# Cosformer attention and a multiplicative feed-forward layer on one core: the output products of tiles 2 to 8 by seven block products in place of eight

## The chip, the cores and the metric

The kernel runs on one core of one Trainium2 chip, as one launch. The metric is the device time of that core in microseconds (us). The kernel before takes 253.65 us (median of 3 runs, 253.58 to 253.87). The span of a profile is a little shorter than the time, as it runs from the first to the last instruction.

## The reference

The first part is linear attention with cosine weights, of 8 batches, 8 heads, 576 positions and 64 features a head. The second is a feed-forward layer on the 4608 rows that result, with 512 columns in and out and 1024 inside.

```python
# attention, for each batch and head; c, s = cos, sin of pi/2 * position / 576
phi = lambda x: concatenate([relu(x) * c, relu(x) * s], axis=-1)
kv  = einsum('bhsf,bhsd->bhfd', phi(k), v)
num = einsum('bhsf,bhfd->bhsd', phi(q), kv)
den = einsum('bhsf,bhf->bhs', phi(q), phi(k).sum(axis=2)) + 1e-6
x   = (num / den)  # as 4608 rows of 512
# feed-forward
out = (((x @ w1) * (x @ w2)) @ w3) @ w_out
```

Inputs and output are float32; the kernel multiplies in bfloat16 and accumulates in float32.

## The kernel before

The kernel forms w34 = w3 @ w_out once on the chip, so the layer is out = ((x @ w1) * (x @ w2)) @ w34. The rows are worked off in nine tiles t = 0 to 8 of 512 rows. A tile first has eight pairs of products (index jc, 128 of the 1024 inner columns each): ScalarE copies the first of a pair from PSUM, VectorE multiplies it with the second into abT. Then comes the output stage of four row blocks `ms` of 128 rows. Tiles 0 and 1 have a variant of the first stage that is cut here.

```python
def ffn_tile():                                  # four PSUM banks, taken in turn
    pool = ps_ffn[ffn_tiles[0] // 2 % 2]         # two pools, bufs=2 each
    ffn_tiles[0] += 1
    return pool.tile([P, 512], FP32, name="ffnps")

def ffn_groups(t):
    abT = fsb.tile([P, 8, 512], BF16, name="abT", bufs=2)
    ...
    for jc in range(4 if t < 2 else 0, 8):
        aT = ffn_tile()
        products(aT[:, :], w1b, jc, slice(0, 512))       # 4 matmuls of 512 columns, L432
        asb = fsb.tile([P, 512], BF16, name="asb")
        nc.scalar.copy(out=asb[:], in_=aT[:, :])         # L469
        yield
        bT = ffn_tile()
        products(bT[:, :], w2b, jc, slice(0, 512))
        nc.vector.tensor_mul(out=abT[:, jc, :], in0=asb[:], in1=bT[:, :])   # L473
        yield
    ...
    for ms in range(3 if t == NT - 1 else 4):            # the output stage
        ops = ffn_tile()
        for jc in range(8):
            nc.tensor.matmul(ops[:, :], lhsT=abT[:, jc, ts(ms, 128)], rhs=w34b[:, jc, :],
                             start=(jc == 0), stop=(jc == 7))               # L486
            if jc == 3:
                yield
        if ms % 2 == 0:
            osb = holds[0].tile([P, 2, 512], FP32, name="osb")
            kept.append(osb)
        nc.scalar.copy(out=osb[:, ms % 2, :], in_=ops[:, :])                # L493
        if t == NT - 1:
            store(nc.sync, osb[:, ms % 2:ms % 2 + 1, :], 4 * t + ms, 1)
        yield
    # the last block of the last tile: two halves of 256 columns (L502), each stored at once
```

At each `yield` the program puts the attention work of later rows that the plan has for this slot: features of q and k (L259 on VectorE, L263 on ScalarE), the copy of v (L283, GpSimd), kv (L291), the numerators (L349) and their normalization on VectorE. A tile from t = 1 on has 24 slots: two for each jc and eight in the output stage. Every engine works its instructions off in the order in which the program gives them. The accumulators `pnum` of kv and of the numerators have one buffer of two banks. Attention ends with tile 6.

```python
def num(b, c, chain=True):
    ...
    nt = ps_att.tile([P, 2, 512], FP32, name="pnum")     # ps_att: bufs=1
    for h in range(H):
        nc.tensor.matmul(nt[:, h // 4, ds((h % 4) * 65, 65)], lhsT=qpT[:, h, ds(at, 128)],
                         rhs=kvs[:, h, :], start=True, stop=True)           # L349
    ...
    def normalize():
        nc.vector.tensor_scalar_add(out=den[rows], in0=n4[:, :, :, 64], scalar1=1e-6)   # L359
        nc.vector.reciprocal(out=den[rows], in_=den[rows])                              # L360
        nc.vector.tensor_tensor(out=xblk[rows], in0=n4[:, :, :, 0:D], in1=..., op=ALU.mult)  # L361

bases = [74, 99, 123, 148, 173]                          # slots of batches 4 to 7
for b, last, base in zip(range(4, B), bases, bases[1:]):
    plan_loads(b, [last + s for s in (-8, -5, 1, 4, 7, 10)])
    plan(b, kf=[last + s for s in (4, 7, 10, 13, 15)],   # features of k
         vc=[base + s for s in (-9, -8, -7, -6, -5)],    # copies of v
         kv=[base + s for s in (-4, -3, -3, -2, -2)],
         qf=[base + s for s in (-12, -9, -6, -3, 0)],    # features of q
         nu=[base + s for s in (0, 2, 5, 8, 11)])        # numerators
```

The outputs stay in the ten buffers `osb` (HELD) until their store is issued by GpSimd, at planned slots. Loads and stores on GpSimd come behind a small copy (`seen`, L521) that waits for a mark of ScalarE (L519), which keeps them from starting early.

Of the kernel before, what the change touches and what calls it, by code (L numbers as in the profile page):

```python
# [68 lines left out]
def kernel(  # L69
# [11 lines left out]
    nc = tc.nc  # L81
# [4 lines left out]
    NT = T // 512  # L86

    const = ctx.enter_context(tc.tile_pool(name="const", bufs=1))
# [46 lines left out]
    w34b = const.tile([P, 8, DM], BF16, name="w34b")  # L135
# [255 lines left out]
    def rows_of(b, c, n):  # L391

        if b == 0:
            if c == 4:
                return [out[512:S, :].rearrange("(p j) m -> p j m", j=1)]
            return [out[0:512, :].rearrange("(p j) m -> p j m", j=4)[:, c:c + n, :]]
        lower = out[ds(b * S, 320), :].rearrange("(p j) m -> p j m", j=5)
        upper = out[ds(b * S + 320, 256), :].rearrange("(p j) m -> p j m", j=4)
        return [h[:, c:c + n, :] for h in ((lower,) if c == 4 else (lower, upper))]

    def store(eng, osb, g, n, cols=slice(0, DM)):

        pair, r = divmod(g, 9)
        b, c = (2 * pair, r) if r < 4 else (2 * pair + 1, r - 5)
        if r == 4:
            parts = rows_of(2 * pair, 4, 1) + rows_of(2 * pair + 1, 4, 1)
        elif n == 1 or c + n <= 4:
            parts = rows_of(b, c, n)
        else:
            parts = None  # L410
        if parts is None or (r == 4 and n > 1):
            for i in range(n):
                store(eng, osb[:, i:i + 1, :], g + i, 1, cols)
            return
        for i, rows in enumerate(parts):
            on = eng[i % 2] if isinstance(eng, tuple) else eng
            on.dma_start(out=rows[:, :, cols], in_=osb[64 * i:64 * i + rows.shape[0], :, cols])  # L417

    ffn_tiles = [0]

    def ffn_tile():
        pool = ps_ffn[ffn_tiles[0] // 2 % 2]
# [4 lines that stand above are left out]
        x = xT[t]  # L427
        abT = fsb.tile([P, 8, 512], BF16, name="abT", bufs=2)

        def products(out, w, jc, tok):  # L430
            for kc in range(4):
                nc.tensor.matmul(out, lhsT=w[:, kc, ts(jc, 128)], rhs=x[:, kc, tok],  # L432
                                 start=(kc == 0), stop=(kc == 3))

        def on_half(half):

            for pair in range(2):
                a, b = ffn_tile(), ffn_tile()
                if pair == 0 and t == 0:
                    for quarter in range(2):  # L440
                        for i in range(2):
                            for ps, w in ((a, w1b), (b, w2b)):
                                products(ps[:, ds(256 * i + 128 * quarter, 128)], w, i,
                                         ds(256 * half + 128 * quarter, 128))
                            if half == 0 and quarter == 0 and i == 0:
                                yield
                        if quarter == 0:
                            yield
                else:
                    for ps, w in ((a, w1b), (b, w2b)):  # L450
                        for i in range(2):
                            products(ps[:, ts(i, 256)], w, 2 * pair + i, ts(half, 256))
                        if w is w1b and (t == 1 or half == 0):
                            yield
                asb = fsb.tile([P, 512], BF16, name="asb")
                nc.scalar.copy(out=asb[:], in_=a[:, :])
                nc.vector.tensor_mul(out=abT[:, ts(pair, 2), ts(half, 256)],
                                     in0=asb[:].rearrange("p (i n) -> p i n", i=2),
                                     in1=b[:, :].rearrange("p (i n) -> p i n", i=2))
                yield  # L460

        if t < 2:
            yield from on_half(0)
            yield from on_half(1)
        for jc in range(4 if t < 2 else 0, 8):
            aT = ffn_tile()
            products(aT[:, :], w1b, jc, slice(0, 512))
# [3 lines that stand above are left out]
            bT = ffn_tile()  # L471
            products(bT[:, :], w2b, jc, slice(0, 512))
            nc.vector.tensor_mul(out=abT[:, jc, :], in0=asb[:], in1=bT[:, :])  # L473
            yield
        if t == 0:
            for jp in range(8):
                for part in range(2):
                    w34_mm(jp, part)
                    yield
            early.close()  # L480
            holds.append(ctx.enter_context(tc.tile_pool(name="hold", bufs=HELD,
                                                        reuse_waits="tile")))
        for ms in range(3 if t == NT - 1 else 4):
            ops = ffn_tile()
            for jc in range(8):
# [12 lines that stand above are left out]
            for half in range(2):  # L498
                cols = ts(half, 256)
                ops = ffn_tile()  # L500
                for jc in range(8):
                    nc.tensor.matmul(ops[:, 0:256], lhsT=abT[:, jc, ts(3, 128)],  # L502
                                     rhs=w34b[:, jc, cols], start=(jc == 0), stop=(jc == 7))
                nc.scalar.copy(out=osb[:, 1, cols], in_=ops[:, 0:256])
                store((nc.sync, nc.scalar), osb[:, 1:2, :], 4 * t + 3, 1, cols)
                yield


    HELD = 10
    holds, kept = [], []  # L510
    slots = [[] for _ in range(40 + 24 * (NT - 1))]

    def at(s, *calls):
        slots[s] += calls

    def hold_back():

        mark = sm.tile([P, 1], BF16, name="mark", bufs=8)
        nc.scalar.copy(out=mark[0:1, :], in_=zeros[0:1, 0:1])  # L519
        seen = sm.tile([P, 1], BF16, name="seen", bufs=1)  # L520
        nc.gpsimd.tensor_copy(out=seen[0:1, :], in_=mark[0:1, :])  # L521
# [13 lines left out]
    def plan_loads(b, when):  # L535

        for piece, s in zip([(n, half) for n in "kqv" for half in range(2)], when):
            def issue(piece=piece):
                hold_back()
                load(b, *piece)  # L540
            at(s, issue)
# [57 lines left out]
    for b, last, base in zip(range(4, B), bases, bases[1:]):  # L599
        plan_loads(b, [last + s for s in (-8, -5, 1, 4, 7, 10)])  # L600
        plan(b, kf=[last + s for s in (4, 7, 10, 13, 15)],
             vc=[base + s for s in (-9, -8, -7, -6, -5)],
             kv=[base + s for s in (-4, -3, -3, -2, -2)],
             qf=[base + s for s in (-12, -9, -6, -3, 0)],
             nu=[base + s for s in (0, 2, 5, 8, 11)])

    for i in range(2 * (NT - 1)):
        def put(i=i):
            hold_back()
            store(nc.gpsimd, kept[i][:, :, :], 2 * i, 2)  # L610
# [3 lines left out]
    for t in range(NT):  # L614
        for _ in ffn_groups(t):
            for u in slots[g]:
                u()
            g += 1
# [31 lines left out]
```

## Time and profile before

| | before |
|---|---|
| time | 253.65 us (253.58 to 253.87) |
| span of the profile | 251.3 us, granted TensorE clock 1.00 |
| TensorE, VectorE, ScalarE, GpSimd busy | 240.8, 139.0, 130.5, 94.3 us |
| output products L486, L502 | 271 recorded of 280, and 16 |
| output stages of tiles 2 to 8 begin at | 103.6, 127.1, 150.8, 174.2, 197.9, 219.4, 239.9 us |
| spans of tiles 2 to 8 | 23.4, 24.0, 23.7, 23.3, 23.3, 20.9, 25.1 us |

The spans are cut where the first products of each tile begin, at 87.6, 111.0, 135.0, 158.7, 182.0, 205.3 and 226.2 us; that of tile 8 has the end of the program in it. In the profile PE is TensorE, PEld its weight loads, DVE VectorE, ACT ScalarE, POOL GpSimd; L486 is line 486 of the kernel. A group's row has the number of instructions, their busy time, the mean duration of one in ns, and the idle time of the engine just before them with what ended it. Durations of matmuls overlap, so the pace of matmuls is taken from the distance of their starts. The slices divide the span into forty parts, each digit the busy share in tenths.

### The profile page before, as it was taken

The numbers are of one execution on the slowest core, as the hardware profiler recorded it, in microseconds if no ns is written. First come the engines' busy times: TensorE is split into PE (matmuls) and PEld (weight loads), VectorE is DVE, ScalarE is ACT, GpSimd is POOL, SyncE is SP. The second block draws the span as 40 slices with busy tenths as digits, with TensorE's granted clock in tenths as the row PEclk, the third lists the DMA queues.
The fourth block names the chain that finished last, engine by engine and source line by source line (L and its number), as shares of the span: only waits on it lengthen the run. The fifth ranks groups of instructions, "written<-read, shape, count | busy, mean of one in ns | idle before, by whom it ended". The sixth has DMA issues, their size and how long they took to land.

```text
span 251.3 us, 5013 instructions
## 1 busy us (share of the span) xinstructions
PE 240.8 (96%) x1838; PEld 130.7 (52%) x1867; DVE 139.0 (55%) x331; ACT 130.5 (52%) x269; POOL 94.3 (38%) x197
## 2 busy tenths in 40 slices
PE   8889999999999999999999999999999999999993
PEld 2578555565874445454544545454545444444442
DVE  7775663637878445649565475567475644303310
ACT  2676324686843783466556644854575333334322
POOL 7764240232242344128032712382233009785000
PEclk9999999999999999999999999999999999999999
DMA  6999999899999999999999999999998447997015
GB/s 194 185 194 200 210 204 204 112 121 148 140 146 183 176 148 138 145 149 166 154 179 181 187 136 174 189 168 143 187 172 162 95 45 194 273 314 246 0 42 125
DMA packets 83895, 41.02 MB, mean 163 GB/s; under 512 B 51488, under 2 KB 80416, under 8 KB 83872
## 3 DMA queue, kind: packets, MB, share of 16 engines
q0 software_dynamic: 35456, 27.20, 70.4%
q1 hardware_dynamic: 48256, 13.38, 37.6%
q8 instruction: 14, 0.23, 0.4%
q10 hardware_dynamic: 160, 0.13, 0.2%
q14 instruction: 9, 0.07, 0.1%
HBM read 38.80 MB, written 9.44 MB: 192 GB/s over the span
## 4 chain that ended last, share of the span: by engine, by line
PE 77%; DMA 13%; DVE 4%; issue 2%; POOL 1%; ACT 1%; ACTq 0%; POOLq 0%; DVEq 0%
PE ffnps L432 41%; PE ffnps L486 24%; DMA w3b<-in_moe_w_dram 6%; PE pnum L349 4%; PE pnum L291 4%; PE ffnps L226 3%; DMA w2b<-in_moe_w_dram 3%; DMA qs<-in_q_dram 3%; DVE xblk L361 2%; DVE abT L473 1%; PE pst L214 1%; PE pst L322 1%; DVE den L360 1%; PE pst L387 0%; DVE qp L259 0%
## 5 line engine op out<-in xcount | busy, mean ns | idle before, releaser
L432 PE MATMUL ffnps<-xT,w2b 128*128 128x512 bf16 (+2 forms) x332 | 74.6, 348 | 0.3
L432 PE MATMUL ffnps<-xT,w1b 128*128 128x512 bf16 (+2 forms) x323 | 73.6, 347 | 0.8 <-DVE xT L389 0.3
L473 DVE TENSOR_TENSOR abT<-asb,ffnps 128x512 bf16<-128x512 bf16 x64 | 43.9, 686 | 48.4 <-PE ffnps L432 46.1
L469 ACT CAST asb<-ffnps 128x512 bf16<-128x512 f32 x64 | 37.3, 583 | 52.5 <-PE ffnps L432 48.7
L486 PE MATMUL ffnps<-w34b,abT 128*128 128x512 bf16 x271 | 63.7, 379 | 0.5
L521 POOL COPY seen<-mark 1x1 bf16<-1x1 bf16 x52 | 10.3, 197 | 96.8 <-ACT mark L519 96.8
L432 PEld LDWEIGHTS <-w1b 128*128 128x128 bf16 x336 | 30.4, 98 | 26.8 <-issue 0.8
L432 PEld LDWEIGHTS <-w2b 128*128 128x128 bf16 x336 | 30.5, 98 | 26.6
L486 PEld LDWEIGHTS <-abT 128*128 128x128 bf16 x280 | 26.1, 98 | 28.2 <-DVE abT L473 0.2
L493 ACT COPY osb<-ffnps 128x512 f32<-128x512 f32 x35 | 20.5, 585 | 35.4 <-PE ffnps L486 35.3
L263 ACT ACTIVATE qp<-qs,sinv 128x512 bf16<-128x512 bf16 (+2 forms) x40 | 28.0, 715 | 1.6 <-DMA qs<-in_q_dram 1.6
L361 DVE TENSOR_TENSOR xblk<-pnum,den 128x512 bf16<-128x512 f32 (+1 forms) x39 | 26.9, 691 | 1.4
L263 ACT ACTIVATE kp<-ks,sinv 128x512 bf16<-128x512 bf16 (+1 forms) x35 | 24.8, 717 | 2.6 <-DMA ks<-in_k_dram 2.6
L417 POOL DMA_DIRECT2D out_dram<-osb x42 | 22.3, 536 | 3.4 <-issue 3.0
L283 POOL COPY va<-vs 128x512 bf16<-128x512 bf16 (+1 forms) x30 | 17.8, 629 | 11.9 <-DMA vs<-in_v_dram 11.9
L259 DVE TENSOR_SCALAR qp<-qs,cosv 128x512 bf16<-128x512 bf16 (+1 forms) x40 | 19.4, 493 | 2.8 <-DMA qs<-in_q_dram 2.8
L349 PEld LDWEIGHTS <-qpT 128*128 128x128 bf16 x320 | 14.9, 98 | 10.1 <-issue 1.9
L359 DVE TENSOR_SCALAR den<-pnum 128x8 f32<-128x8 f32 (+1 forms) x39 | 6.4, 164 | 24.3 <-PE pnum L349 24.2
L349 PE MATMUL pnum<-kvs,qpT 128*128 128x65 bf16 x312 | 16.4, 194 | 0.7 <-DVE xblk L361 0.3
L226 PE MATMUL ffnps<-woutb,w3T 128*128 128x512 bf16 x62 | 14.8, 379 | 0.1
L291 PEld LDWEIGHTS <-kp 128*128 128x128 bf16 x280 | 11.4, 98 | 4.1
L259 DVE TENSOR_SCALAR kp<-ks,cosv 128x512 bf16<-128x512 bf16 (+1 forms) x35 | 12.0, 353 | 2.5 <-DMA ks<-in_k_dram 2.5
(83 smaller groups left out, 180.0 us busy)
## 6 DMA issues: line engine op xcount, KB each, us to landing
out_dram<-osb POOLq DMA_DIRECT2D x16, 256.0 KB, 4.4
out_dram<-osb POOLq DMA_DIRECT2D x24, 128.0 KB, 3.7
qs<-in_q_dram POOLq DMA_DIRECT2D x9, 256.0 KB, 7.9
ks<-in_k_dram POOLq DMA_DIRECT2D x7, 320.0 KB, 6.9
qs<-in_q_dram POOLq DMA_DIRECT2D x7, 320.0 KB, 6.9
vs<-in_v_dram POOLq DMA_DIRECT2D x7, 320.0 KB, 6.5
ks<-in_k_dram POOLq DMA_DIRECT2D x7, 256.0 KB, 7.8
vs<-in_v_dram POOLq DMA_DIRECT2D x7, 256.0 KB, 5.5
```

The costliest lines, as they stand in the source:

```text
L226: nc.tensor.matmul(acc[:, :], lhsT=w3T[:, lc, :], rhs=woutb[:, lc, :], start=(lc == 0), stop=(lc == 7))
L259: nc.vector.tensor_scalar(out=dst[:R, c, :, 0:D], in0=src[:R, :, c, :], scalar1=0.0, scalar2=cosv[:R, at:at + 1], op0=ALU.max, op1=ALU.mult)
L263: nc.scalar.activation(out=dst[:R, c, 0:n, D:F], in_=src[:R, 0:n, c, :], func=ACTF.Relu, scale=sinv[:R, at:at + 1], bias=0.0)
L291: nc.tensor.matmul(kvt[:, h // 4, ds((h % 4) * 65, 65)], lhsT=kp[:, c, h, :], rhs=va[:, c, h, 0:D + 1], start=(i == 0 and h % 4 == 0), sto ...
L349: nc.tensor.matmul(nt[:, h // 4, ds((h % 4) * 65, 65)], lhsT=qpT[:, h, ds(at, 128)], rhs=kvs[:, h, :], start=True, stop=True)
L361: nc.vector.tensor_tensor(out=xblk[rows], in0=n4[:, :, :, 0:D], in1=den[rows].unsqueeze(3).to_broadcast([R, 2, 4, D]), op=ALU.mult)
L417: on.dma_start(out=rows[:, :, cols], in_=osb[64 * i:64 * i + rows.shape[0], :, cols])
L432: nc.tensor.matmul(out, lhsT=w[:, kc, ts(jc, 128)], rhs=x[:, kc, tok], start=(kc == 0), stop=(kc == 3))
L469: nc.scalar.copy(out=asb[:], in_=aT[:, :])
L473: nc.vector.tensor_mul(out=abT[:, jc, :], in0=asb[:], in1=bT[:, :])
L486: nc.tensor.matmul(ops[:, :], lhsT=abT[:, jc, ts(ms, 128)], rhs=w34b[:, jc, :], start=(jc == 0), stop=(jc == 7))
L493: nc.scalar.copy(out=osb[:, ms % 2, :], in_=ops[:, :])
```

## The change

One level of Strassen's scheme is put on the output product of tiles 2 to 8. The four row blocks of a tile are taken as two pairs (a = 0, 1). For each pair abT is a matrix of two by two blocks (rows 0 and 1 of the pair; inner columns 0 to 511 and 512 to 1023), and w34 is one of two by two blocks (inner rows; output columns 0 to 255 and 256 to 511). Eight block products of 4 matmuls of 256 columns each would be what the kernel before computes; the scheme needs seven, of sums of blocks, and adds the results up. It is for less work on TensorE; sums take its place on the other engines:

- five sums of blocks of w34 (`wsum`), once, by VectorE, in tile 2;
- sums of blocks of abT in each tile, behind jc = 1, 3 (GpSimd, from tile 7 on VectorE) and behind jc = 5, 6, 7 (VectorE), two of them in place;
- sums of the products for each pair, on VectorE out of PSUM, and for tiles before 7 two subtractions on GpSimd. Three of the seven products are accumulated in the PSUM bank of an earlier one after that has been read.

The number of slots of a tile stays. The diff, with blank lines and the passage that gives each product its operands cut:

```diff
+    wsum = {i: const.tile([P, 4, 256], BF16, name=f"wsum{i}") for i in (1, 3, 4, 6, 7)}
+    asum = {i: const.tile([P, 4, 2, P], BF16, name=f"asum{i}") for i in (1, 5, 6)}
...
+    def product_sums(t, abT, lo, hi):
+        v = abT[:].rearrange("p j (a h n) -> p j a h n", a=2, h=2)
+        a11, a21 = (v[:, lo % 4:(hi - 1) % 4 + 1, :, h, :] for h in range(2))
+        a12, a22 = (v[:, 4 + lo % 4:4 + (hi - 1) % 4 + 1, :, h, :] for h in range(2))
+        n = slice(lo % 4, (hi - 1) % 4 + 1)
+        if lo < 4:
+            eng = nc.gpsimd if t < BUSY else nc.vector
+            eng.tensor_tensor(out=asum[6][:, n], in0=a21, in1=a11, op=ALU.subtract)
+            return
+        for out, in0, in1, op in ((asum[1][:, n], a11, a22, ALU.add),
+                                  (asum[5][:, n], a11, a12, ALU.add),
+                                  (a21, a21, a22, ALU.add), (a12, a12, a22, ALU.subtract)):
+            nc.vector.tensor_tensor(out=out, in0=in0, in1=in1, op=op)
...
+            b3, b6 = ffn_tile(), ffn_tile()
+            product(b3, 3, True)
+            nc.scalar.copy(out=c12, in_=b3[:, 0:256])
+            product(b6, 6, True)
+            yield
+            b4, b1 = ffn_tile(), ffn_tile()
+            product(b4, 4, True)
+            add(c11, c12, b4[:, 0:256])
+            product(b1, 1, True)
+            add(c22, c11, b1[:, 0:256])
+            yield
+            product(b3, 5, False)
+            nc.scalar.copy(out=c12, in_=b3[:, 0:256])
+            put(0, ts(1, 256))
+            product(b4, 2, False)
+            nc.scalar.copy(out=c21, in_=b4[:, 0:256])
+            put(1, ts(0, 256))
+            if t < BUSY:
+                add(c11, c11, c12, ALU.subtract, nc.gpsimd)
+                add(c22, c22, c21, ALU.subtract, nc.gpsimd)
+            else:
+                add(c11, c11, b3[:, 0:256], ALU.subtract)
+                add(c22, c22, b4[:, 0:256], ALU.subtract)
+                add(c22, c22, b6[:, 0:256])
+                put(1, ts(1, 256))
+            yield
+            product(b1, 7, False)
+            add(c11, c11, b1[:, 0:256])
+            put(0, ts(0, 256))
+            if t < BUSY:
+                add(c22, c22, b6[:, 0:256])
+            yield
...
+            if by_seven(t) and jc in (1, 3, 5, 6, 7):
+                product_sums(t, abT, jc - (jc < 6), jc + 1)
...
+        if by_seven(t):
+            yield from out_by_seven(t, abT)
+            return
...
+    SEVEN, BUSY = 2, 7
...
+    for i, s in zip((3, 6, 4, 1, 7), (66, 68, 70, 73, 76)):
+        at(s, lambda i=i: weight_sum(i))
```

`product` is four matmuls of 256 columns, `add` one sum of 128 x 256 float32 on VectorE unless an engine is named, `put` stores a piece in the last tile and does nothing before it, and `by_seven(t)` is true from tile 2 on. `weight_sum` is one VectorE instruction on two blocks of w34 of 128 x 1024.

More of the change, by code (lines that the diff above doesn't have):

```diff
@@ L417, in store, with w34_block, weight_sum @@
             on.dma_start(out=rows[:, :, cols], in_=osb[64 * i:64 * i + rows.shape[0], :, cols])
+    wsum = {i: const.tile([P, 4, 256], BF16, name=f"wsum{i}") for i in (1, 3, 4, 6, 7)}
+    asum = {i: const.tile([P, 4, 2, P], BF16, name=f"asum{i}") for i in (1, 5, 6)}
+    def w34_block(row, col):
+        return w34b[:, ts(row, 4), ts(col, 256)]
+    def weight_sum(i):
+        (r0, c0), (r1, c1), op = {1: ((0, 0), (1, 1), ALU.add), 3: ((0, 1), (1, 1), ALU.subtract),
+                                  4: ((1, 0), (0, 0), ALU.subtract), 6: ((0, 0), (0, 1), ALU.add),
+                                  7: ((1, 0), (1, 1), ALU.add)}[i]
+        nc.vector.tensor_tensor(out=wsum[i][:], in0=w34_block(r0, c0), in1=w34_block(r1, c1), op=op)
@@ new lines, in by_seven @@
+    def by_seven(t):
+        return t >= SEVEN
+    def product_sums(t, abT, lo, hi):
[11 more added lines that the diff above has]
+            nc.vector.tensor_tensor(out=out, in0=in0, in1=in1, op=op)
@@ new lines, in out_by_seven, with lhs, product, put @@
+    def out_by_seven(t, abT):
+        w = {1: wsum[1], 2: w34_block(0, 0), 3: wsum[3], 4: wsum[4], 5: w34_block(1, 1),
+             6: wsum[6], 7: wsum[7]}
+        for a in range(2):
+            def lhs(i, kc):
+                if i in (1, 5, 6):
+                    return asum[i][:, kc, a, :]
+                row, h = {2: (0, 1), 3: (0, 0), 4: (4, 1), 7: (4, 0)}[i]
+                return abT[:, row + kc, ts(2 * a + h, P)]
+            def product(ps, i, begin):
+                for kc in range(4):
+                    nc.tensor.matmul(ps[:, 0:256], lhsT=lhs(i, kc), rhs=w[i][:, kc, :],
+                                     start=(begin and kc == 0), stop=(kc == 3),
+                                     skip_group_check=True)
+            osb = holds[0].tile([P, 2, 512], FP32, name="osb")
+            kept.append(osb)
+            c11, c12 = osb[:, 0, 0:256], osb[:, 0, 256:512]
+            c21, c22 = osb[:, 1, 0:256], osb[:, 1, 256:512]
+            last = t == NT - 1
+            def put(h, cols):
+                if last:
+                    store((nc.sync, nc.scalar), osb[:, h:h + 1, :], 4 * t + 2 * a + h, 1, cols)
+            def add(out, in0, in1, op=ALU.add, eng=nc.vector):
+                eng.tensor_tensor(out=out, in0=in0, in1=in1, op=op)
+            b3, b6 = ffn_tile(), ffn_tile()
[30 more added lines that the diff above has]
+            yield
@@ L509 @@
     HELD = 10
+    SEVEN, BUSY = 2, 7
+    assert SEVEN > 1
     holds, kept = [], []
```

## The prediction

> **What bounds the kernel now.** I read the busy line and the slices of the page first, then the table of windows for the stretches of tiles 2 to 8, then the costliest groups, and last the chain and the VectorE timeline inside one tile.
>
> ```profile
> PE 240.8 (96%) x1838; PEld 130.7 (52%) x1867; DVE 139.0 (55%) x331; ACT 130.5 (52%) x269; POOL 94.3 (38%) x197
> PE   8889999999999999999999999999999999999993
> DVE  7775663637878445649565475567475644303310
> ...
> L473 DVE TENSOR_TENSOR abT<-asb,ffnps 128x512 bf16<-128x512 bf16 x64 | 43.9, 686 | 48.4 <-PE ffnps L432 46.1
> ...
> L486 PE MATMUL ffnps<-w34b,abT 128*128 128x512 bf16 x271 | 63.7, 379 | 0.5
> ```
>
> TensorE is full from slice 4 to the end, and the output products (L486) wait 0.5 us in all. So TensorE sets the time, and 1 us of matmul taken out is worth up to 1 us. VectorE is at 55%, and its product of a and b (L473) mostly waits for TensorE. That looks like room, but it is an average. The table of windows, one row for each of tiles 3 and 4:
>
> ```profile
> 111.00:135.00 24.00, 23.59 (x182) 11.95 (x182) 16.50 (x37) 14.01 (x31) 8.79 (x19) 1.00 1.26 163
> 135.00:158.70 23.70, 23.40 (x174) 11.90 (x177) 13.92 (x35) 13.90 (x30) 8.85 (x19) 1.00 1.30 174
> ```
>
> The columns are span, then busy PE, PEld, DVE, ACT, POOL. VectorE is busy for 16.5 of 24.0 us in tile 3, because attention for later tiles runs between. In tile 7 (205.30 to 226.20), without attention, it is 6.47 of 20.90. The chain inside tile 3 says more:
>
> ```profile
> 121.14 1.74 PE ffnps L432 x8
> ...
> 122.97 0.69 DVE abT L473
> 123.66 0.26 DVE qp L259
> ...
> 124.26 0.70 DVE xblk L361
> 124.96 0.14 issue
> 125.10 0.42 PE pnum L349 x8
> ```
>
> The last product pairs of a tile are already closed by VectorE: product 5 (L473), then a feature, then the normalization (L359 to L361); only then may TensorE start the next attention numerator at 125.10, since pnum has one buffer. The same pattern stands at 146.82 in tile 4 and at 195.43 in tile 6. Anything put on VectorE ahead of that normalization delays TensorE one for one.
>
> **What the Trainium skill says.** TensorE: Matmul & The Clock Gate, "Wait — 56ns, not 53.3ns?", gives a matmul its column count over 2.4 GHz plus about 2.5 ns. The trace agrees: 24 products of 512 columns take 5.18 us in the chain (216 ns each), and eight of 256 take 0.87 us at 62.41 (109 ns each), with a weight load for each. So half-width products lose almost nothing. VectorE: DVE Perf Modes, "The perf-mode tier table", lets an add of two bf16 operands in SBUF run at double rate and one with a PSUM operand only at single rate. The trace has the second (686 ns for 512 elements, about 150 ns of it fixed), not the first; from the page's figures I estimate 420 ns for 512 and 290 ns for 256 elements in SBUF, and 420 ns for 256 elements with an f32 PSUM operand. GPSIMD Engine Reference, "3.1 Elementwise", makes an elementwise pair some two times slower there than on VectorE; here a plain copy of 512 elements takes 623 ns, so I estimate 0.7 us for a subtraction of 256 f32. SBUF — State Buffer, "Who interferes with whom", has a VectorE instruction with two SBUF inputs exclude a GpSimd one that reads SBUF. The trace shows the same kind of exclusion: a qp feature that usually takes 0.35 us took 1.79 us at 164.58, while GpSimd copied va.
>
> **The change part by part.** *Removed on TensorE:* of each of seven tiles 32 products of 512 columns, 32 x 0.216 = 6.91 us. *Added:* 2 x 7 x 4 = 56 products of 256 columns, 56 x 0.109 = 6.10 us. That is 0.81 us a tile, 5.7 us in all (2.2%), and 248.0 us is the floor if everything else hides.
>
> *Added on VectorE, sums of products:* behind product 5 four sums of 512 elements, behind 6 and 7 four of 256 each. In the timeline an instruction starts about 0.09 us before the end of an independent one, so I count 0.33 and 0.20 us: 1.3 + 0.8 + 0.8 = 2.9 us a tile. *Sums of outputs:* four f32 sums with a PSUM operand for each of two halves, 8 x 0.42 = 3.4 us a tile. Tiles 7 and 8 add the sums that GpSimd has before. *Once:* five weight sums of 1024 elements, some 3 us, in tile 2. So VectorE in tile 3 goes from 16.5 to 22.8 us of 24. ScalarE swaps four copies of 512 (585 ns) for six of 256 (372 ns): nothing. GpSimd gets two sums of 512 and four subtractions of 256 a tile, some 5 us, queued with its DMA issues (0.68 us each).
>
> *What lies on the path.* I laid out tile 3 by hand, with zero at 122.70, where the products of jc=5 end. VectorE, in program order:
>
> - product 5 at 0.27 to 0.87, its sums to 2.2, qp feature to 2.5, normalization to 3.5 (2.26 before);
> - product 6 to 4.1, sums to 4.9, normalization to 6.0, product 7 to 6.6, the first of its sums to 6.8, all to 7.4;
> - kp feature to 7.8, the normalization of the next chunk to 8.9, then the first output sums, c11 to 9.3 and c22 to 9.8.
>
> TensorE against that: the numerator that stood at 2.4 starts at 3.65 (the first 1.3 us lost). Products of jc=7 end at 5.7; block products 3 and 6 need only early operands and end at 6.5, a numerator at 6.8. Block product 4 finds product 7 just ready, and 4, 1 and 5 run to 8.1. Block product 2 goes into the bank that the c11 sum must first read: 9.4 (1.3 us lost). Then 7 ends at 10.3, a numerator at 10.6, product 3 of the second half at 11.0. Its product 6 needs the bank of the first half's product 6, which is free only after: ScalarE copies c21 (10.3), GpSimd subtracts twice (11.3), VectorE adds twice (11.8). It starts at 11.9 (0.9 lost), and the half ends at about 14.8. Before, the stage ended at 12.2. So tile 3 gets 2.6 us longer, and the second product of the next tile may wait some 0.5 us more for that same bank.
>
> The same layout gives about 2.8 us for tile 2 (a weight sum in place of the feature) and for tile 4, 2.0 for tile 5, whose numerators fall better, and 2.2 for tile 6: with tile 3 some 12.6 us. In tile 7 there is no attention: product 7 is done 0.7 us after the last pair, hidden behind block products 3 and 6, and only some 0.2 us is lost, so 0.6 us is won. Tile 8 wins about 0.2, since its last output now ends in a queue of sums instead of one copy of 0.37 us. Sum: 253.65 + 12.6 - 0.8 = 265.4 us.
>
> **The rivals.** *First: all is hidden.* VectorE is free nearly half the time, the order 3, 6, 4, 1 was chosen to give its sums time, and the intervals for reusing a bank (0.9 us) exceed one sum (0.42). Then the time is 248 to 250 us. For it: tile 7 shows nothing in the way. Against it: the chain of tiles 3, 4 and 6, where VectorE already holds TensorE. *Second: GpSimd's part is the wait.* Its subtractions stand behind DMA issues and exclude VectorE's sums; then every half waits 1 us or more longer than I count, and the time goes to 268 us or more. The wait of TensorE would end on GpSimd's output or on the c22 sum in tiles 2 to 6. *Third: only the waits for banks count,* because the sums of products find gaps; then tiles 2 to 6 lose about 1 us each and the time is about 257 us. *Fourth: the store tail grows,* as 256-column pieces are stored at the end; it is worth tenths of a us.
>
> **Range and chances.** The hand layout gives 265.4 us. It treats each tile as starting without slack and counts two waits at full length where a delayed TensorE may give VectorE time to catch up; I take off about a quarter of the 11.8 us and say 262.5. The lower edge, 251, leaves room for the first rival with small waits; the upper, 269, for the second. Within 2% means 248.6 to 258.7 us; faster by over 2% requires practically the whole ideal gain, so 0.05; within 2% 0.25, mostly for the third rival; slower 0.70.
>
> **What would show it.** Right: VectorE at 75 to 80% of the span, sums of 512 at about 0.42 us; matmuls of 256 columns 109 ns apart inside a product; TensorE's idle time ending on abT, xblk and the output sums, 2 us or more in each of tiles 2 to 6, and tile 7 shorter by about 0.6 us than its 20.9. Wrong: if the spans of tiles 3 to 6 fall below 23.7 us, VectorE's queue was not the limit, and I have taken overlapping work for serial; if the sums take 690 ns, the loss is greater; if the largest wait ends on GpSimd, the second rival holds.

## The result and the profile after

The changed kernel takes 276.18 us (276.02 to 276.24) against 253.62 us before: ratio 1.0887, 95% interval 1.0868 to 1.0906, some 22.6 us slower. The prediction said 262.5 us, with a range up to 269; the direction was right, the size less than half.

The page after has, in the same order as the lines shown of before, the busy line, two rows of slices and rows of the groups:

```profile
PE 243.5 (89%) x2027; PEld 146.8 (54%) x2027; DVE 196.1 (72%) x488; ACT 130.2 (47%) x282; POOL 120.4 (44%) x227
PE   8889999999999997899779977998899879999972
DVE  6875735658774799577977797669789965774763
...
L477 DVE TENSOR_TENSOR osb<-osb,ffnps 128x256 f32<-128x256 f32 x64 | 26.2, 418 | 14.2 <-POOL osb L477 3.6
...
L477 POOL TENSOR_TENSOR osb<-osb 128x256 f32<-128x256 f32 x20 | 14.2, 727 | 30.6 <-DVE osb L477 22.6
...
L349 PE MATMUL pnum<-kvs,qpT 128*128 128x65 bf16 x312 | 16.4, 194 | 8.1 <-DVE xblk L361 6.7
```

VectorE has 57 us more to do, TensorE has holes in the slices that were full, and numerators (L349) wait 8.1 us, which hardly waited in the page before:

```profile
L349 PE MATMUL pnum<-kvs,qpT 128*128 128x65 bf16 x312 | 16.4, 194 | 0.7 <-DVE xblk L361 0.3
```

The waits of TensorE (us in total, times, longest):

```profile
PE ffnps L462 <- DVE osb L477: 8.5, 12, 1.1
PE pnum L349 <- DVE xblk L361: 6.7, 5, 2.0
PE ffnps L525 <- ACT asb L562: 1.3, 2, 0.7
```

Two waits stand out: the block products (L462) for output sums, the numerators for the normalization. The distance from a tile's first product to the next tile's, read from the TensorE timeline (for tile 8 up to the end of the span), shows where the time went. The table has it for all runs below, from one profile each. (For `before` it is cut at the first matmul of each tile, so its spans differ by up to 0.3 us from those ahead of the prediction.)

| us | t1 | t2 | t3 | t4 | t5 | t6 | t7 | t8 | ratio to before (95%) |
|---|---|---|---|---|---|---|---|---|---|
| before | 25.17 | 23.66 | 23.86 | 23.59 | 23.28 | 23.34 | 20.98 | 25.18 | |
| after | 25.61 | 28.76 | 27.20 | 27.36 | 27.39 | 25.71 | 22.07 | 27.70 | 1.0887 (1.0868 to 1.0906) |
| floor | 26.13 | 25.41 | 24.54 | 22.81 | 22.48 | 22.55 | 21.27 | 27.41 | 0.998 (0.995 to 1.001) |
| no_psums_subs | 26.82 | 25.54 | 23.69 | 24.44 | 24.75 | 23.72 | 21.27 | 27.87 | 1.029 (1.021 to 1.037) |
| no_psums | 25.86 | 25.37 | 24.72 | 25.01 | 25.45 | 24.16 | 21.84 | 27.95 | 1.038 (1.034 to 1.043) |
| no_subs | 26.17 | 27.38 | 26.17 | 26.78 | 27.07 | 25.24 | 21.28 | 28.15 | 1.068 (1.060 to 1.076) |
| no_gpsimd | 26.66 | 26.87 | 26.42 | 26.15 | 26.30 | 26.72 | 21.26 | 27.48 | 1.064 (1.060 to 1.069) |
| before_plus_sums | 25.24 | 25.01 | 25.15 | 25.06 | 24.67 | 24.44 | 20.97 | 25.20 | 1.024 (1.017 to 1.030) |
| order | 25.35 | 27.81 | 26.94 | 27.10 | 27.37 | 25.68 | 22.08 | 27.87 | 1.081 (1.074 to 1.088) |
| banks | 26.17 | 27.99 | 26.17 | 26.14 | 26.72 | 24.07 | 20.71 | 27.48 | 1.060 (1.054 to 1.067) |
| banks_order | 25.15 | 26.77 | 25.92 | 25.89 | 26.72 | 24.06 | 20.73 | 27.98 | 1.056 (1.048 to 1.063) |
| no_wsums | 26.69 | 27.35 | 26.98 | 27.35 | 27.73 | 25.70 | 21.85 | 27.54 | 1.079 (1.071 to 1.087) |
| seven_from7 | 28.24 | 23.66 | 23.69 | 24.10 | 23.27 | 23.35 | 21.27 | 27.45 | 1.013 (1.006 to 1.020) |
| seven_from7_sync | 25.92 | 23.66 | 23.81 | 23.91 | 23.28 | 23.33 | 21.28 | 29.81 | 1.020 (1.012 to 1.028) |
| seven_only7 | 25.97 | 23.66 | 24.13 | 23.97 | 23.27 | 23.34 | 21.28 | 25.22 | 1.003 (0.999 to 1.006) |
| even_banks | 25.94 | 23.66 | 24.40 | 23.60 | 23.28 | 23.33 | 20.36 | 27.32 | 1.005 (1.003 to 1.008) |
| even_banks_stores | 26.09 | 23.66 | 23.94 | 23.60 | 23.28 | 23.33 | 20.36 | 26.43 | 1.001 (0.998 to 1.004) |
| only7_banks | 25.83 | 23.66 | 23.69 | 23.93 | 23.27 | 23.34 | 20.36 | 25.19 | 0.996 (0.993 to 0.999) |
| seven_and_half | 25.32 | 23.66 | 23.69 | 23.89 | 23.28 | 23.33 | 20.37 | 25.82 | 1.002 (0.999 to 1.004) |

After minus before: +5.1, +3.3, +3.8, +4.1, +2.4 in tiles 2 to 6, +1.1 in tile 7, +2.5 in tile 8, 0.4 in tile 1, together the 22.7 us. The experiments ran on other chips, where single times of the kernel before spread from 253 to 259 us and tile 1, with its transfers, varies between runs; so ratios are to the kernel before on the same chip, and I compare tiles, not totals, where less than 2 us matter.

### The profile page after: what moved, and what is told of

The parts are those of the page before. It is cut to its first block, busy times and chain, and to the rows that moved or that the text cites. A ratio compares the mean times of both kernels' runs of the same rounds, so it can differ in the third digit from the quotient of the medians.

```text
span 274.2 us, 5624 instructions
## 1 busy us (share of the span) xinstructions
PE 243.5 (89%) x2027; PEld 146.8 (54%) x2027; DVE 196.1 (72%) x488; ACT 130.2 (47%) x282; POOL 120.4 (44%) x227
## 3 DMA queue, kind: packets, MB, share of 16 engines
q0 software_dynamic: 35456, 27.20, 65.2%
## 5 line engine op out<-in xcount | busy, mean ns | idle before, releaser
L525 PE MATMUL ffnps<-xT,w1b 128*128 128x512 bf16 (+2 forms) x336 | 75.0, 348 | 0.3 <-DVE xT L389 0.3
L477 DVE TENSOR_TENSOR osb<-osb,ffnps 128x256 f32<-128x256 f32 x64 | 26.2, 418 | 14.2 <-POOL osb L477 3.6
L477 POOL TENSOR_TENSOR osb<-osb 128x256 f32<-128x256 f32 x20 | 14.2, 727 | 30.6 <-DVE osb L477 22.6
L462 PEld LDWEIGHTS <-abT 128*128 128x128 bf16 x224 | 21.5, 99 | 10.9 <-issue 5.1
L462 PE MATMUL ffnps<-wsum,abT 128*128 128x256 bf16 x168 | 25.3, 276 | 0.6 <-DVE abT L566 0.6
L259 DVE TENSOR_SCALAR qp<-qs,cosv 128x512 bf16<-128x512 bf16 (+1 forms) x40 | 24.1, 611 | 2.1 <-DMA qs<-in_q_dram 2.1
L283 POOL COPY va<-vs 128x512 bf16<-128x512 bf16 (+1 forms) x30 | 18.9, 659 | 11.1 <-DMA vs<-in_v_dram 8.4
L349 PE MATMUL pnum<-kvs,qpT 128*128 128x65 bf16 x312 | 16.4, 194 | 8.1 <-DVE xblk L361 6.7
L349 PEld LDWEIGHTS <-qpT 128*128 128x128 bf16 x320 | 14.8, 98 | 15.4 <-issue 7.8
L462 PE MATMUL ffnps<-wsum,asum 128*128 128x256 bf16 x112 | 17.3, 278 | 5.3 <-DVE osb L477 5.3
L462 PEld LDWEIGHTS <-asum 128*128 128x128 bf16 x168 | 16.7, 100 | 9.6 <-issue 7.4
L491 ACT COPY osb<-ffnps 128x256 f32<-128x256 f32 x14 | 5.2, 372 | 27.7 <-DVE osb L477 18.9
```

The costliest lines, as they stand in the source:

```text
L259: nc.vector.tensor_scalar(out=dst[:R, c, :, 0:D], in0=src[:R, :, c, :], scalar1=0.0, scalar2=cosv[:R, at:at + 1], op0=ALU.max, op1=ALU.mult)
L283: eng.tensor_copy(out=feat_of(b)[2][:R, c, :, 0:D], in_=raw[b, "v"][:R, :, c, :])
L462: nc.tensor.matmul(ps[:, 0:256], lhsT=lhs(i, kc), rhs=w[i][:, kc, :], start=(begin and kc == 0), stop=(kc == 3), skip_group_check=True)
L477: eng.tensor_tensor(out=out, in0=in0, in1=in1, op=op)
```

## The experiments

The theories that the expectations name: A, VectorE's sums of blocks stand in its queue ahead of what TensorE waits for; B, the output sums, with GpSimd in their chain, hold the PSUM banks; D, for tile 8, ScalarE's queue stands behind the issue of stores.

**What the parts cost.** All four leave out some of the sums in tiles 2 to 6, so they don't compute the layer; they only show what the parts cost. `floor` has no sums there and four plain copies as output:

```diff
# floor, tiles 2 to 6: raw blocks as operands; the products as in the change, in four banks
-                add(c11, c12, b4[:, 0:256]) ... add(c22, c22, b6[:, 0:256])
+                nc.scalar.copy(out=c11, in_=b6[:, 0:256])
+                nc.scalar.copy(out=c12, in_=b3[:, 0:256])   # c21 from b4, c22 from b1
# no_psums
+        if t < BUSY:
+            return          # in product_sums, behind the GpSimd part; products 1, 5 take a11
# no_subs
-                add(c11, c11, c12, ALU.subtract, nc.gpsimd)
-                add(c22, c22, c21, ALU.subtract, nc.gpsimd)
# no_psums_subs: both
```

> Tiles 2 to 6 multiply the raw blocks seven times with no sums of blocks of abT and with four plain ScalarE copies as output (the result is not the reference's); tiles 7 and 8 and the weight sums stay. If all of the loss of tiles 2 to 6 comes from the sums, each of them falls 0.8 us below its span before, and with tile 7 at -0.5 and tile 8 at +2.6 us as now the time is about 251.7 us. If narrow products themselves are slow for TensorE (issue, weight loads, clock), it stays above 256 us.

> VectorE's twelve sums of blocks of abT are left out in tiles 2 to 6, their products take raw blocks (the result is not the reference's); everything else stays. Theory A (VectorE's queue: the sums stand ahead of the normalization that TensorE waits for): the waits of 1.6 to 2.0 us for xblk go, the slow clock in tile 2 with them, and the output sums are reached earlier: about 264 us. Theory B (the output sums and GpSimd hold the banks): less than 4 us is won, above 272 us.

> The two GpSimd subtractions of each half are left out in tiles 2 to 6 (the result is not the reference's), the VectorE sums stay. Theory B: the waits of the second half's product 6 and of the next tile's second product, together some 1.6 us a tile, mostly go: about 268 us. Theory A alone: 274 us or more.

> Both left out in tiles 2 to 6: VectorE's sums of blocks of abT and GpSimd's subtractions (the result is not the reference's). If A and B are two separate waits, the gains add: about 256 to 258 us. If one only hides the other, it is no better than the better of the two alone.

In `floor` tiles 4 to 6 take 22.81, 22.48 and 22.55 us, each 0.8 us less than before. (At the end of tile 2 its profile has a wait of 2.4 us for a transfer of x, which the other runs don't have, and in tile 3 the granted clock is 0.50 for some 3.5 us; these two tiles are left aside. The ratio of 0.998 is 253.2 us, above the 251.7 us expected; in how many runs that wait came isn't known.) So narrow block products are as cheap as the prediction took them, and the whole loss of tiles 4 to 6 is in the sums and the waits that they bring. The time of tiles 4, 5 and 6 together, step by step: before 70.2; floor 67.8; with the VectorE output sums (`no_psums_subs`) 72.9; with GpSimd's subtractions too (`no_psums`) 74.6; with the sums of blocks of abT (after) 80.5. Per tile: 0.8 won, then 1.7, 0.6 and 1.9 us lost. On the scale of 253.6 us the ratios are 263.3 us for `no_psums`, where theory A expected 264, and 270.9 for `no_subs`, where theory B expected 268: A was met, B in this form was too big. The two parts nearly add: the subtractions cost 0.6 us a tile without the other sums and 0.5 with them. `no_psums_subs` still came to 260.9 us, not to the 256 to 258 us expected, since the output sums on VectorE that stay in it cost 1.7 us a tile.

**The sums alone, and their place.** `before_plus_sums` is the kernel before with the twelve VectorE sums added; `order` is the changed kernel with those behind jc = 5 and 6 issued after the attention work of the slot.

```diff
# before_plus_sums: behind the product of a and b, into a buffer that nothing reads
+            if 2 <= t < 7 and jc in (5, 6, 7):
+                product_sums(abT, jc - (jc < 6), jc + 1)
# order
-            if by_seven(t) and jc in (1, 3, 5, 6, 7):
+            if by_seven(t) and jc in (1, 3, 7):
                 product_sums(t, abT, jc - (jc < 6), jc + 1)
             yield
+            if by_seven(t) and jc in (5, 6):
+                product_sums(t, abT, jc - (jc < 6), jc + 1)
```

> The kernel before, with the changed kernel's twelve VectorE sums of blocks of abT added in tiles 2 to 6 at the same places (into a scratch buffer that nothing reads); TensorE's work is that of before. Theory A: the sums alone delay the normalization and so TensorE; in the changed kernel they cost tiles 4 to 6 about 1.9 us each, so 5 x 1.5 to 2 us: 261 to 264 us. If they only cost together with the output sums behind them, less than 3 us: below 257 us.

> The changed kernel with the same work; only the sums behind jc=5 and jc=6 are issued after the attention work of their slot, not before it. If it is the place in VectorE's queue that costs (theory A as an order), the waits for xblk of 1.6 to 2.0 us shrink to under 0.5 us, and 5 to 7 us of the 22 come back: about 270 us. If it is VectorE's amount of work up to the output stage, the wait only moves to the block products 1 and 4, and the time stays at 275 to 277 us.

The added sums alone make the kernel before 1.024 times as long, 1.1 to 1.5 us in each of tiles 2 to 6, with TensorE's work unchanged. That is 259.6 us, less than the 261 to 264 us expected: in tiles 4 to 6 the sums cost 1.3 us each here and 1.9 in the changed kernel, so a third of their price comes only with the output sums behind them. Its waits of TensorE have one new line of weight:

```profile
PE pnum L349 <- DVE xblk L361: 6.1, 5, 1.7
```

That is the four sums behind jc = 5, 4 x 0.34 us, put straight ahead of a normalization. It says the prediction's first step was right. But `order`, which takes just these and the ones behind jc = 6 out of the way, gains next to nothing in tiles 4 to 6 (80.2 against 80.5 us); most of its gain (1.081 against 1.089) is in tile 2, where the slow clock told of below did not come. The TensorE timeline of tile 3 in `order` (start, duration, the wait in brackets):

```profile
130.03 0.42 PE L349 MATMUL pnum<-kvs,qpT 128*128 128x65 bf16 x8 [0.25 <-DVE xblk L361]
...
134.32 0.28 PE L462 MATMUL ffnps<-wsum,abT 128*128 128x256 bf16 x1 [0.57 <-DVE abT L566]
...
136.87 0.60 PE L462 MATMUL ffnps<-w34b,abT 128*128 128x256 bf16 x4 [1.39 <-DVE osb L477]
```

The numerator's wait fell from 1.72 to 0.25 us, as expected; the time came back ahead of block product 4, which waits for the last product of a and b (0.57), and of block product 2 (1.39 against 1.03). VectorE's backlog has to be worked off before c11 is there, in either order. So theory A holds as an amount of work between jc = 5 and the first output sum, not as an order.

**The banks and GpSimd's chain.** `banks` gives block product 6 a bank of its own, out of two that nothing uses after batch 1; `no_gpsimd` lets VectorE do all sums.

```diff
# banks
-            b3, b6 = ffn_tile(), ffn_tile()
+            b3 = ffn_tile()
+            b6 = ps_tr.tile([P, 512], FP32, name="pst")
# banks_order: banks and order; no_gpsimd
-    SEVEN, BUSY = 2, 7
+    SEVEN, BUSY = 2, 2
```

> The changed kernel with block product 6 in a bank of its own, one of two that the transposes of batches 0 and 1 have left free, so neither the next half nor the next tile waits for the last c22 sum. Theory B: the waits of 0.7 to 1.0 us before product 6 of the second half and before the next tile's second product go, some 1.5 us a tile: about 268 us, and tile 7 falls below its 21.0 us before. If VectorE's backlog is what TensorE waits for, the wait moves to product 2: above 273 us.

> Both: the later place of the sums behind jc=5 and 6 and the bank of its own for product 6. If both theories hold and are separate, the gains add: about 262 us. If VectorE is simply full (20.9 to 23.5 us busy in tiles of 27 us), it stays above 268 us.

> The changed kernel with all sums on VectorE, GpSimd doing none, in every tile. If GpSimd's part (its chain of two subtractions of 0.73 us, and its exclusion of VectorE) is what hurts, the time falls by 3 us or more, below 273 us on the quiet chip. If VectorE is the bound of tiles 2 to 6, its further 2.5 us a tile add up: 280 us or more.

`banks` comes to 1.060: tiles 4 to 6 fall by 3.5 us together, 1.2 a tile where 1.5 were expected, and tile 7 falls below before, to 20.71 us. The TensorE waits in tile 3 are now a numerator of 1.71 and product 2, twice:

```profile
131.93 0.42 PE L349 MATMUL pnum<-kvs,qpT 128*128 128x65 bf16 x8 [1.71 <-DVE xblk L361]
...
137.55 0.60 PE L462 MATMUL ffnps<-w34b,abT 128*128 128x256 bf16 x4 [1.03 <-DVE osb L477]
...
141.46 0.60 PE L462 MATMUL ffnps<-w34b,abT 128*128 128x256 bf16 x4 [0.34 <-DVE osb L477]
```

The waits ahead of product 6 and of the next tile are gone; theory B holds for the bank. With `order` on top next to nothing more is won in tiles 3 to 6 (0.5 us together), and 262 us, expected if the two gains add, was missed.

`no_gpsimd` is faster than the change (1.064 against 1.089; 269.9 us on the scale of 253.6), below the 273 us that were set as the mark for GpSimd's part being what hurts, with VectorE 203.0 us busy instead of 196.1 and its waits for output sums down from 8.5 to 6.6 us:

```profile
PE ffnps L462 <- DVE osb L477: 6.6, 14, 1.1
PE pnum L349 <- DVE xblk L361: 5.9, 5, 1.9
PE ffnps L525 <- DVE abT L566: 1.1, 1, 1.1
```

VectorE adding straight from PSUM (416 ns) is quicker than a ScalarE copy (372 ns) and a GpSimd subtraction of 727 ns in a row, for the bank that is waited for; and without GpSimd the kernel adds product 6 to c22 before block product 7, not after it, which also frees that bank earlier. Besides, GpSimd's sums hold VectorE up. The features of q and k together (L259, 128 x 512, 60 of them) have a mean of 447 ns before, 535 after and 442 without GpSimd's sums; and one weight sum took 2.21 us where the other four took about 0.69, while GpSimd copied v and summed blocks. The same weight sum took 1.16 us in `floor`, where GpSimd sums nothing in that tile. How much each of these effects is worth these runs don't tell.

**The weight sums.** `no_wsums` takes raw blocks of w34 in their place, so it doesn't compute the layer.

```diff
-    for i, s in zip((3, 6, 4, 1, 7), (66, 68, 70, 73, 76)):
-        at(s, lambda i=i: weight_sum(i))
```

> The changed kernel without the five weight sums: raw blocks of w34 take their place (the result is not the reference's). Tile 2 lost 5.3 us where tiles 3 to 6 lost 3.3 to 4.1. If the weight sums on VectorE make the difference (two of them took 0.68 us, one 2.21 beside GpSimd) and bring the clock down by the longer wait, tile 2 falls to the level of tile 3: about 274 us. If not, the time stays at 276 us.

Tile 2 falls from 28.76 to 27.35 us, within 0.4 us of tile 3, and the time to 1.079 (273.7 us), as expected. Part of what tile 2 lost before was the clock, which no step of the prediction had. The table of windows of the changed kernel, after the wait of 1.97 us in tile 2 (the column of 1.00, 0.77, 0.50, 0.50, 0.52 is the granted clock):

```profile
106.00:107.00 1.00, 0.53 (x11) 0.54 (x12) 1.00 (x3) 0.00 (x0) 0.00 (x0) 1.00 0.71 50
107.00:108.00 1.00, 1.00 (x9) 0.83 (x8) 0.96 (x5) 0.64 (x3) 0.05 (x1) 0.77 1.18 152
108.00:109.00 1.00, 1.00 (x7) 0.69 (x6) 0.93 (x4) 0.44 (x1) 0.75 (x2) 0.50 1.12 185
109.00:110.00 1.00, 1.00 (x7) 0.69 (x6) 0.89 (x4) 0.00 (x0) 0.08 (x1) 0.50 0.42 18
110.00:111.00 1.00, 1.00 (x6) 0.74 (x5) 0.28 (x2) 0.37 (x1) 0.11 (x1) 0.52 0.66 54
```

Sixteen block matmuls took 3.4 us there instead of 1.7. `banks` has the same dip behind the same wait of 1.97 us. But `no_subs`, with the weight sums and a wait of the same length there, has none:

```profile
106.80 0.42 PE L349 MATMUL pnum<-kvs,qpT 128*128 128x65 bf16 x8 [1.98 <-DVE xblk L361]
...
108.00:109.00 1.00, 1.00 (x11) 0.90 (x10) 0.93 (x6) 0.77 (x3) 0.48 (x2) 1.00 1.42 203
```

Nor have `no_wsums` (a wait of 1.35 us) and `no_gpsimd` (1.94 us). So the 1.4 us of `no_wsums` hold the weight sums and the dip, and the dip doesn't follow from the length of the wait alone. From tile 2 of `order` and `banks_order`, which have the weight sums and no dip, I estimate 0.7 to 1.0 us for the dip: they gain 0.95 and 1.2 us there on `after` and `banks`, and 0.3 in tile 3. Where nothing else is added to VectorE in tile 2, the weight sums cost nothing: 23.66 us as before, in all seven runs below.

**Tiles 7 and 8.** The prediction had them win 0.8 us; they lost 3.6.

```diff
# seven_from7
-    SEVEN, BUSY = 2, 7
+    SEVEN, BUSY = 7, 7
# seven_from7_sync: and
-                    store((nc.sync, nc.scalar), osb[:, h:h + 1, :], 4 * t + 2 * a + h, 1, cols)
+                    store(nc.sync, osb[:, h:h + 1, :], 4 * t + 2 * a + h, 1, cols)
# seven_only7
-        return t >= SEVEN
+        return t == 7
```

> Seven products only in tiles 7 and 8, which have no attention beside them; weight sums stay in tile 2. By the prediction's own sum the two tiles win 0.8 us: about 252.8 us. By the profile after, tile 7 wins 0.5 and tile 8 loses 2.6 us, and the weight sums cost tile 2 a little: about 256 us.

> As seven_from7, with the stores of the last tile all issued by SyncE, none by ScalarE. Theory D (ScalarE's queue stands behind the issue of stores that wait for VectorE, so its copies of the second half come late): tile 8 gets back some 2 us, about 254 us or less. Rival: the chain of VectorE's sums at the end sets the tail, then within 0.5 us of seven_from7.

> Seven products in tile 7 alone, tile 8 by eight products as before. Tile 7 wins 0.5 us, tile 2 pays for the weight sums up to 1 us: 253.1 to 254.1 us.

Tile 7 takes 21.3 us in all three, 0.3 more than before: its 0.8 us are eaten by waits even with no attention beside it. By the distance of starts in `seven_only7` these are 0.5 us ahead of product 6 of the second half, 0.2 ahead of product 2, 0.2 at the start of the next tile and 0.1 each ahead of two more products. Part of tile 7's loss in the changed kernel is the wait that tile 6 leaves behind. Tile 8 ends late in `seven_from7` as in the change, and later still with SyncE alone, where theory D expected 2 us back. The timeline of the changed kernel's last tile:

```profile
262.78 0.37 ACT L491 COPY osb<-ffnps 128x256 f32<-128x256 f32 x1 [1.44 <-DVE osb L477]
...
263.18 0.57 ACTq L417 DMA_DIRECT2D out_dram<-osb  x1
...
264.20 2.56 ACTq L417 DMA_DIRECT2D out_dram<-osb  x3
...
265.13 0.60 PE L462 MATMUL ffnps<-wsum,asum 128*128 128x256 bf16 x4 [0.74 <-DVE osb L477]
...
266.88 0.37 ACT L481 COPY osb<-ffnps 128x256 f32<-128x256 f32 x1 [2.71 <-DMA out_dram<-osb]
...
267.30 0.60 PE L462 MATMUL ffnps<-w34b,asum 128*128 128x256 bf16 x4 [0.70 <-ACT osb L481]
```

ACTq is ScalarE issuing stores. Three of them stand in its queue and wait for VectorE's sums; the copy of the second half's first product, ready at 264.4, waits behind them until 266.88, and VectorE and TensorE with it. With all stores on SyncE TensorE needs 21.0 us for tile 8 up to its last matmul instead of the 22.1 of `seven_from7`, so theory D holds for it; but sixteen stores of half rows keep SyncE issuing for 10.12 us, 0.63 each from start to start, long after VectorE's last sum, and the end moved out by 2.4 us.

Two more runs undo these waits without changing the work: sums spread evenly, product 6 in its own bank, and stores of whole rows:

```diff
# even_banks: as banks, from tile 7 on, and
-            if by_seven(t) and jc in (1, 3, 5, 6, 7):
-                product_sums(t, abT, jc - (jc < 6), jc + 1)
+            if by_seven(t) and jc in (1, 3, 4, 5, 6, 7):
+                product_sums(t, abT, jc - (jc < 4), jc + 1)
# even_banks_stores: and, in the last tile, row 1 of a pair when c22 is done, row 0 when
# c11 is done, by SyncE; row 0 of the last pair in two pieces, the last over SyncE and ScalarE
# only7_banks: as even_banks, with
+        return t == 7
# seven_and_half: as even_banks_stores, the last pair of tile 8 by eight, as before the change
```

> Seven products only in tiles 7 and 8, with three changes of timing but none of work: a bank of its own for block product 6, and the sums of blocks spread one jc at a time behind jc=4 to 7; the stores of the last tile as in the change. If bank reuse and VectorE's four sums behind jc=5 are what ate tile 7's gain, its span falls from 21.3 us (seven_from7) to about 20.2, and the last tile still ends late: some 255 us against 254.5 of before on this chip.

> As even_banks, with the stores of the last tile reordered: whole rows by SyncE as soon as both halves are there, only the very last piece split over SyncE and ScalarE, so ScalarE's copies wait for no store. Theory D: the last tile ends 2 to 3 us earlier than in even_banks and 0.5 us or more earlier than in the kernel before; the ratio to before is about 0.994. If the chain of VectorE's last sums and the stores sets the end anyway, the last tile stays at 26 us or more and nothing is won.

> Seven products in tile 7 alone, with the bank of its own for product 6 and the sums spread behind jc=4 to 7; tile 8 as before. Tile 7 takes 20.36 us as in even_banks (20.98 before), all else is as before: 0.6 us less than before, a ratio of 0.9976. If anything of the weight sums or of the changed stores stays on the path, 1.000 or more.

> As only7_banks, and in tile 8 seven products for the first pair of row blocks only; the second pair is multiplied by eight and stored as in the kernel before, so its end is the old one. If the last tile lost by its chain of sums and stores at the end alone, TensorE's gain of 0.4 us comes through: 1.0 us less than before, a ratio of 0.996.

Tile 7 falls to 20.36 us in all four, 0.62 less than before, so the bank and the burst behind jc = 5 had eaten its gain. No run parts the two; by the waits above, some 0.7 us of the 0.9 won against `seven_only7` are the bank's. The stores won 0.9 us of tile 8, less than the 2 to 3 expected. There TensorE is done 20.3 us after the tile began, earlier than before (20.9), but the end is at 26.4: after the last matmul VectorE still has two sums, and SyncE issues its nine stores until about 1.5 us later in the tile than before. In `seven_and_half`, with the old end for the last pair, TensorE needs 20.5 us of tile 8 to its last matmul, the 0.4 less that were expected, but the tile takes 25.82 us against 25.19 in `only7_banks`: what TensorE wins is lost after it, and the ratio is 1.002, not 0.996. SyncE's stores of the last tile, in `seven_and_half` and in `before`:

```profile
243.75 5.19 SPq L417 DMA_DIRECT2D out_dram<-osb  x8
242.47 5.85 SPq L417 DMA_DIRECT2D out_dram<-osb  x8
```

In the tile's own time that is from 17.98 to 23.17 us, and from 16.35 to 22.20 before. The first row is stored only when its last sum is done, 1.6 us later than before, and from then on SyncE issues almost without a break, so the last store is issued at 22.62 us (before 21.65), lands at 24.64 (before 23.97), and the span ends 1.2 us after that in both.

`only7_banks` came out at 0.996 (0.993 to 0.999): the one version whose interval lies below 1, if by less than 1%; by the tile table it wins some 0.6 us, from one tile. It is the seven-product scheme only where nothing else wants VectorE and no store ends the program.

## Why the prediction was wrong in size

**Right.** The bound, TensorE, and the floor of 0.8 us a tile (`floor`). The durations: 421 and 286 ns for sums of 512 and 256 elements in SBUF (estimated 420 and 290), 418 ns for output sums (420), 727 ns on GpSimd (0.7 us). VectorE's 196.1 us are 72% of the longer span, somewhat below the 75 to 80% foreseen. And tile 3's layout by hand, in the TensorE timeline of the changed kernel, where that zero is 128.85:

```profile
132.72 0.42 PE L349 MATMUL pnum<-kvs,qpT 128*128 128x65 bf16 x8 [1.72 <-DVE xblk L361]
...
138.34 0.60 PE L462 MATMUL ffnps<-w34b,abT 128*128 128x256 bf16 x4 [1.03 <-DVE osb L477]
...
140.88 0.60 PE L462 MATMUL ffnps<-wsum,asum 128*128 128x256 bf16 x4 [0.72 <-DVE osb L477]
...
145.67 1.02 PE L525 MATMUL ffnps<-xT,w2b 128*128 128x512 bf16 x4 [0.67 <-ACT asb L562]
```

The layout had these at 3.65, 9.4 and 11.9 after zero, and the end of the stage at 14.8; they came at 3.87, 9.49, 12.03 and 15.1. So the mechanism was right for a tile with attention, and `before_plus_sums` and `banks` confirm two of its three waits, those of the numerator and of product 6's bank.

**Wrong, by steps.** Between 262.5 and 276.2 us lie 13.7 us, by the tile table about 6.1 in tiles 2 to 6, 4.4 in tiles 7 and 8, 2.9 by the quarter taken off, and 0.4 in tile 1. "With tile 3 some 12.6 us" for tiles 2 to 6 came to 18.7 (the terms given add up to 12.4). First, the wait of the next tile's second product (the last line above), which the text gave as 0.5 us more, was never put into the sum; it is 0.29, 0.67, 0.67, 0.30 and 0.41 us at the starts of tiles 3 to 7, 2.3 us in all. In tiles 4 and 5 it ends on ScalarE's copy by name, in the others on VectorE's output sum; in the line shown VectorE's last c22 sum had ended at 145.65, and `banks`, which frees that bank, takes the wait away. Second, tile 2 was put at 2.8 and is 5.1: weight sums beside GpSimd and the slow clock, 1.4 us by `no_wsums`. Third, tile 5, "whose numerators fall better", is 4.1 where 2.0 stood: its numerator waits less (0.78 against 1.72 us in tile 3), but there are waits of 0.67 us at its start, 0.59 for the last product of a and b, 0.98 ahead of product 6 of the second half, and two of 0.2.

"0.6 us is won" in tile 7: 0.3 us was lost without a neighbour's wait. The layout had only some 0.2 us of delay there; in `seven_only7` waits of 1.1 us came, most of them for the bank of product 6, and `even_banks` brought the 0.6 back. "Tile 8 wins about 0.2": it lost 2.5, since the fourth rival, the store tail, was put at tenths of a us and the step did not look at which engine issues the stores. TensorE's last matmul came 1.5 us later in the tile than before, behind ScalarE's copy, and the rest is the longer way from there through the sums and stores.

"I take off about a quarter": no catching up shows, as tiles 2 to 6 lost more than the layout without the discount. VectorE is busy 21.7 of 27.2 us in tile 3, and in `order` a wait taken away came back at the next product. Without that step and with the next tile's waits put in, the layout comes to some 268 us, inside the range. What it lacks to 276 lies mainly in tiles 2, 5, 7 and 8.

**The rivals.** The third, waits for banks alone, was real (1.2 us a tile by `banks`) but only a third of the loss. The second, GpSimd's part, I had set aside; taking GpSimd out gives back about 6 us of 22 on the ratio scale (1.064 against 1.089), though VectorE gets more to do: 0.8 to 1.9 us in each of tiles 2 to 5 (tile 2 with the slow clock of the changed kernel in it) and 0.8 in tile 7, while tile 6 takes 1.0 us more. That run also has the earlier sum of product 6 in it. In the largest waits the releaser is VectorE, so the profile's names alone would not have told it.

## What to carry over

Before work is moved off the bound engine, look at the engine that gets it tile by tile, not at its share of the span, and lay out one tile in program order with what each sum must wait for; then add every wait of that layout to the sum, also those that fall into the next tile, and don't discount them without a reason in the profile. A bank or buffer that is read last by the end of a chain of engines delays the bound engine by the whole chain: a spare bank, or a shorter chain with more work on one engine, can be worth more than spreading the work. And stores should not be issued by an engine whose next instruction the critical path needs; nor should one engine get so many at the end that issuing them becomes the path.

## What was not expected of the hardware

The granted clock of TensorE fell to 0.50 for some 3.5 us after a wait of 1.97 us in tile 2 (`after` and `banks`) and one of 2.38 us (`floor`), but not after waits of 1.98 us (`no_subs`) and 1.94 us (`no_gpsimd`), nor after those of 1.6 to 1.7 us in tiles 3 and 4. What decides it these runs don't show. GpSimd held up VectorE visibly in sums, not only in the features where the kernel before showed it: 2.21 us for a sum of 1024 elements that took 0.69 us otherwise. Issuing a store took ScalarE 0.50 to 0.57 us for most stores of the last tile, on top of any wait for its data, and its next copy started only behind the issues (266.88, where its input was ready at 264.4).
